# Strassen's scheme for v and u of the first batch in the second MLP

## The chip, the cores and the metric

One Trainium2 chip, one of its cores. The metric is the device time of one execution in microseconds (us), the median of several runs. The engines of the core are named as the profile names them: PE (matmuls) with PEld (its weight loads), DVE (VectorE), ACT (ScalarE), POOL (GpSimd) and SP, which issues DMAs.

## The reference

Four batches of 576 tokens go through causal attention with decay (8 heads of 64), a first MLP (512 to 2048 to 512, with a layer norm before and a residual), and a second MLP, which is what the change touches:

```python
def _moe2_ref(x, w_in, w_spatial, b_spatial, w_out):
    h = np.maximum(x @ w_in, 0.0)                     # 576 x 1024 per batch
    u, v = (h[..., :512], h[..., 512:])
    mu = np.mean(v, axis=-1, keepdims=True)
    var = np.mean((v - mu) ** 2, axis=-1, keepdims=True)
    v_n = (v - mu) / np.sqrt(var + 1e-06)
    v_s = np.einsum('ts,bsd->btd', w_spatial, v_n) + b_spatial[None, :, None]
    return ((u * v_s) @ w_out).astype(np.float32)
```

## The kernel before

Every large product is made of float16 halves: a float32 matrix X is scaled by a power of two and split into X = Xh + Xl, both float16 (`halves`, L933: one ACT instruction writes the high half, one DVE instruction the low half), and `mm3` (L799) makes three matmuls of each block, Ah·Bl, Al·Bh and Ah·Bh.

The first MLP runs in eight groups of tokens; its last group (blocks 7 and 8, 512 columns a matmul, 16 steps of 24 matmuls) runs from about 492 to 575 us. Beside its matmuls, `load_m2` (L947) loads and splits what the second MLP needs: w_in (its v half first, then its u half; raw in the tile `win`), the first 512 tokens of batch 0 (`load_x2(0)`, L990; raw `x2r`, halves `x2h` and `x2l`), w_spatial (`load_ws`; raw tile `wsr`, halves `wsh` and `wsl`) and w_out (raw `wor`, halves `woh` and `wol`). At its end it forms the four sums of blocks of w_in's u half that Strassen's scheme wants (L981 to L988: four DVE additions, then four splits, into `wuh` and `wul`).

`mlp2(b)` (L1089) is the second MLP of one batch. For batch 0 it makes, in this order: v of tokens 0 to 511 in four tiles of 128 tokens (`vtile`, 12 matmuls of 512 columns each, a ReLU on ACT, mean and variance on DVE, the reciprocal root on ACT and DVE, normalisation on DVE, split into `vh` and `vl`); u transposed, as 4 x 12 matmuls of 288 columns and 4 x 12 of 224 (`utile`, each with a ReLU on ACT); then the last 64 tokens, whose x comes late from the last group (the "tail": `split(ts)`, whose squares stand behind the last ReLU of u on ACT, `self.urelu`); v of the tail (tile 4) and u of the tail (4 x 12 matmuls of 64 columns); the spatial product z (`main`: per half of the tokens 4 x 12 matmuls of 288 columns, whose first 3 read v tile 0, the next 3 tile 1, and so on, and 2 more matmuls each for the tail and the bias); the gate, a product of u and z on DVE; and the output product with w_out. In batches 1 to 3 u already comes from `uunit` (L1143): two units of seven products of 2 x 3 matmuls of 288 columns each, in four PSUM banks A, D, B, C, three of which are used twice, with three copies on ACT and five sums on DVE per unit; the sums of blocks of x are made in `load_x2`, `whole`.

`run` interleaves the steps of the batches: after step n of `mlp2(b)`, `XN[b]` says how many steps of `load_x2(b + 1)` follow; `NEXT` steps of batch 0 run before two steps (`FILL`) of batch 1. What the code writes in this order is a priority: a planner at compile time orders the queue of each engine by it, taking, of what it holds to be ready, what stands first in the code. PSUM banks of the second MLP are taken in the order 2, 3, 4, 7, 0, 1, 5, 6 (`ORDER`).

Of the kernel before, what the change touches and what calls it, by code (L numbers as in the profile page):

```python
# [6 lines left out]
F32 = mybir.dt.float32  # L7
# [36 lines left out]
XN = ((1, 8, 13, 14, 14, 14, 15, 21, 21, 21, 21), (2, 3, 4, 5, 5, 5, 5, 14, 14, 14, 14), (1, 3, 5, 6, 6, 6, 6, 15, 15, 15, 15))  # L44
NEXT, FILL = 22, 2
# [43 lines left out]
class Kernel:  # L89
# [857 lines left out]
    def load_m2(self):  # L947
# [5 lines left out]
        self.undo_in = []  # L953
        for n, hs in enumerate((slice(DM, DF2), slice(0, DM))):
            yield from self.wide([(self.moe2_w_in[k * P : (k + 1) * P, hs], win[:, k, hs]) for k in range(NK)])
            undo, sc = self.scale16([win[:, k, hs] for k in range(NK)], f"win{n}", lambda k: self.wih[:, k, hs], up=3 - n)
            self.undo_in.append(undo)
            sc_u = sc
# [22 lines left out]
        lo, hi, spare = slice(0, 2 * P), slice(2 * P, DM), slice(DM, DF2)  # L981
        s1, s2, s3, s4 = [win[:, i, spare].rearrange("p (k m) -> p k m", k=2) for i in range(4)]
        for out, a, b, op in ((s1, win[:, :2, hi], win[:, 2:, hi], ALU.add), (s2, s1, win[:, :2, lo], ALU.subtract),
                              (s3, win[:, :2, lo], win[:, :2, hi], ALU.subtract), (s4, win[:, 2:, lo], s2, ALU.subtract)):
            nc.vector.tensor_tensor(out=out, in0=a, in1=b, op=op)
        self.wsum = [w.tile([P, 4, 2, 2 * P], F16, name=name) for name in ("wuh", "wul")]
        for i, x in enumerate((s1, s2, s3, s4)):
            self.halves(x, sc_u, self.wsum[0][:, i], self.wsum[1][:, i])  # L988

    def load_x2(self, b):  # L990
# [9 lines left out]
        def split(ts):  # L1000
            behind = (self.tlast if b == 1 else self.glast) if b else self.urelu if undo else None
            g = self.scale16_steps([x2r[:, :, ts]], f"x2s{b % 2}", lambda i: x2h[:, :, ts], behind)
            next(g)
            if b == 1:
                yield
            u, sc = next(g)
            undo.append([self.product(f"x2u{b % 2}{n}", u, self.undo_in[n]) for n in range(2)])
            if b == 1:
                yield
            for k in range(NK):  # L1010
                first = self.halves(x2r[:, k, ts], sc, x2h[:, k, ts], x2l[:, k, ts])
                if b == 0:
                    self.tlast = first
                if b == 1:
                    self.after(first, self.vlast)
                if b == 1 and ts.start == 0 and k < NK - 1:
                    yield

        def whole():
# [9 lines left out]
            a, c = slice(0, S // 2), slice(S // 2, S)  # L1029
            t = self.m2.tile([P, 4, 2, S // 2], F32, tag="x2t", name="x2t", bufs=1)  # L1030
            self.xsum = [self.m2.tile([P, 4, 2, S // 2], F16, tag=tag, name=tag, bufs=1) for tag in ("x2th", "x2tl")]
            for i, (x, y) in enumerate(((x2r[:, :2, c], x2r[:, :2, a]), (x2r[:, 2:, c], t[:, 0]), (x2r[:, 2:, c], x2r[:, :2, c]), (x2r[:, 2:, a], t[:, 1]))):
                self.after(nc.vector.tensor_tensor(out=t[:, i], in0=x, in1=y, op=ALU.subtract), self.gl)
                self.halves(t[:, i], sc, self.xsum[0][:, i], self.xsum[1][:, i])
                yield
# [11 lines left out]
        yield from split(slice(0, 512))  # L1047
        yield
        if b == 0:
            nc.sync.dma_start(out=x2r[:, :, ts], in_=self.tail(self.x2_d, b, N - 512))  # L1050
        yield
        yield from split(ts)

    def load_ws(self):
# [3 lines left out]
        raw = w.tile([P, 5, S], F32, name="wsr")  # L1058
# [30 lines left out]
    def mlp2(self, b):  # L1089
# [22 lines left out]

        def vtile(i):

            lo, hi = i * P, (i + 1) * P
            pv = bank()
# [4 lines left out]
            st = m2.tile([P, 6], F32, tag="bst", name="bst", bufs=3)  # L1121
            mv = m2.tile([P, 2], F32, tag="mv", name="mv", bufs=3)
            y = m2.tile([P, 2], F32, tag="vy", name="vy", bufs=3)
            nc.vector.bn_stats(out=st, in_=v)
            nc.vector.bn_aggr(out=mv, in_=st)
            nc.scalar.activation(y[:, 0:1], mv[:, 1:2], AF.Ln, bias=self.eps)
            nc.scalar.activation(y[:, 0:1], y[:, 0:1], AF.Exp, scale=-0.5)
            nc.vector.tensor_tensor(out=y[:, 1:2], in0=y[:, 0:1], in1=y[:, 0:1], op=ALU.mult)
            nc.vector.scalar_tensor_tensor(out=y[:, 1:2], in0=mv[:, 1:2], scalar=EPS, in1=y[:, 1:2], op0=ALU.add, op1=ALU.mult)
            nc.vector.tensor_scalar(out=y[:, 1:2], in0=y[:, 1:2], scalar1=-0.5, scalar2=1.5, op0=ALU.mult, op1=ALU.add)  # L1130
            nc.vector.scalar_tensor_tensor(out=y[:, 0:1], in0=y[:, 0:1], scalar=2.0**VS, in1=y[:, 1:2], op0=ALU.mult, op1=ALU.mult)
            nc.vector.tensor_scalar(out=v, in0=v, scalar1=mv[:, 0:1], scalar2=y[:, 0:1], op0=ALU.subtract, op1=ALU.mult)
            return v

        def utile(dt, *cols):
            ds_, c0, c1 = slice(dt * P, (dt + 1) * P), cols[0][0], cols[-1][1]
            pu = bank()
            for k in range(NK):
                self.mm3(pu[:, : c1 - c0], self.wih[:, k, ds_], self.wil[:, k, ds_], x2h[:, k, c0:c1], x2l[:, k, c0:c1], k == 0, k == NK - 1)
            for a, e in cols:  # L1140
                self.urelu = nc.scalar.activation(u[:, dt, a:e], pu[:, a - c0 : e - c0], AF.Relu, scale=undo[a // 512][1])

        def uunit(m):  # L1143

            lo, hi = slice(m * P, m * P + P), slice((m + 2) * P, (m + 3) * P)
            t1, t2 = slice(0, HS), slice(HS, S)
            (sh, sl), (th, tl) = self.wsum, self.xsum
            A, D, B, C = [bank()[:, :HS] for _ in range(4)]

            def old(k, ms):  # L1150
                return self.wih[:, k, ms], self.wil[:, k, ms]

            def new(i, k):
                return sh[:, i, k, lo], sl[:, i, k, lo]

            def x(k, ts):
                return x2h[:, k, ts], x2l[:, k, ts]

            def t(i, k):
                return th[:, i, k], tl[:, i, k]  # L1160

            def product(out, w, x, start):
                for k in range(2):
                    self.mm3(out, *w(k), *x(k), start and k == 0, k == 1, skip_group_check=True)

            def part(tag):
                return m2.tile([P, HS], F32, tag=tag, name=tag, bufs=2)

# [361 lines left out]
```

## Time and profile before

| | us |
|---|---|
| median of 3 runs | 771.42 |
| lowest, highest | 769.38, 771.96 |
| the profiled execution | 774.42 |
| its span, first to last instruction | 772.6 |

The time of an execution holds the span and about 1.8 us around it. PE's work is listed twice, as matmuls (PE) and weight loads (PEld). A timeline row gives the start, the time taken (of all instructions merged in the row), engine, line, operation, output and inputs with shapes; a bracket tells the idle time before and what ended it. Where rows overlap, the spacing of their starts is the cost of one more instruction, and the time taken is its latency.

### The profile page before, as it was taken

What the parts mean: (1) busy time and instruction counts of PE and PEld (TensorE: products, weight loads), DVE (VectorE), ACT (ScalarE), POOL (GpSimd) and SP (SyncE); (2) the same over time, 40 slices, a digit from 0 to 9 for tenths busy, and PEclk for the clock granted to TensorE, in tenths of its full rate; (3) what the DMA queues carried; (4) which work ended last, traced back from release to release, by engine and by line L of the source; (5) the groups of instructions that cost most, each with busy time, mean ns of one, the idle gap of its engine ahead of it and who ended that gap; (6) DMA issues with size and microseconds to landing.
All of it is one profiled execution on the core that took longest, in us unless ns stands there. A gap on an engine that the chain in (4) does not pass through costs nothing.

```text
span 772.6 us, 16271 instructions
## 1 busy us (share of the span) xinstructions
PE 747.0 (97%) x5924; PEld 573.0 (74%) x5924; DVE 584.9 (76%) x1549; ACT 528.1 (68%) x1318; POOL 67.2 (9%) x102
## 2 busy tenths in 40 slices
PE   8899998999998999999999999999999999999998
PEld 7788887888876787877878888644447668768676
DVE  7999799576589679979958964779534697785854
ACT  6898599576689588888958853477335765755633
POOL 6001101013101001101200200200012000000000
PEclk9999999999999899999999999999999999999999
DMA  8978793377589799997974874741015230000101
GB/s 264 296 255 295 242 215 71 73 180 124 171 160 170 186 183 174 198 215 159 200 184 102 127 112 143 197 153 56 1 20 110 70 97 28 31 32 1 62 2 62
DMA packets 164099, 104.68 MB, mean 135 GB/s; under 512 B 106146, under 2 KB 151298, under 8 KB 164020
## 3 DMA queue, kind: packets, MB, share of 16 engines
q1 hardware_dynamic: 157784, 96.60, 50.5%
q0 software_dynamic: 5376, 5.54, 5.6%
q10 hardware_dynamic: 860, 1.52, 0.6%
q8 instruction: 46, 0.75, 0.4%
q14 instruction: 33, 0.27, 0.1%
HBM read 64.37 MB, written 15.11 MB: 103 GB/s over the span
## 4 chain that ended last, share of the span: by engine, by line
PE 65%; DVE 13%; ACT 9%; DMA 8%; issue 3%; SPq 1%; DVEq 0%; ACTq 0%
PE ph L858 16%; PE acc L843 13%; PE pb L802 8%; PE pb L803 8%; PE pb L804 8%; PE s L359 3%; PE av L582 2%; DMA vr<-in_v_dram 2%; DMA raw<-in_moe_w_ch_dram 2%; PE s L843 2%; DVE wt L741 1%; DMA raw<-in_moe_w_in_dram 1%; DMA x2z<-decay_d 1%; DVE P L380 1%; ACT P L319 1%
## 5 line engine op out<-in xcount | busy, mean ns | idle before, releaser
L843 PE MATMUL acc<-hh,wt 128*128 128x256 f16 (+2 forms) x960 | 197.6, 296 | 3.0 <-ACT hh L869 2.9
L858 PE MATMUL ph<-xh,wt 128*128 128x256 f16 (+1 forms) x896 | 186.8, 290 | 4.2 <-DVE hl L873 4.1
L858 PEld LDWEIGHTS <-wt 128*128 128x128 f16 x1344 | 127.5, 99 | 50.3 <-issue 12.7
L843 PEld LDWEIGHTS <-wt 128*128 128x128 f16 x1344 | 129.0, 98 | 44.3 <-issue 5.8
L858 PE MATMUL ph<-xl,wt 128*128 128x256 f16 (+1 forms) x448 | 129.6, 289 | 0.0
L843 PE MATMUL acc<-hl,wt 128*128 128x256 f16 (+1 forms) x416 | 116.1, 283 | 0.6 <-DVE hl L873 0.6
L869 ACT ACTIVATE hh<-ph 128x256 f16<-128x256 f32 (+2 forms) x128 | 50.8, 397 | 55.7 <-PE ph L858 55.4
L873 DVE SCALAR_TENSOR_TENSOR hl<-ph,hh 128x256 f16<-128x256 f32 (+1 forms) x112 | 50.7, 454 | 42.2 <-ACT hh L869 41.8
L319 ACT ACTIVATE P<-sd,st 128x512 f16<-128x512 f32 (+1 forms) x128 | 70.0, 585 | 8.5 <-DVE st L370 5.2
L380 DVE SCALAR_TENSOR_TENSOR P<-sd,st,P 128x384 f16<-128x384 f32 (+1 forms) x96 | 58.6, 631 | 11.1 <-ACT P L319 10.2
L367 ACT ACTIVATE sd<-sd,st 128x384 f32<-128x384 f32 (+2 forms) x80 | 54.5, 682 | 13.3 <-DVE st L363 13.1
L359 PE MATMUL s<-x2z 128*128 128x384 f32 (+3 forms) x128 | 48.6, 388 | 6.1 <-DMA x2z<-decay_d 4.2
L363 DVE CUSTOM_DVE_ANT_0 sd<-s,mask 128x384 f32<-128x384 f32 (+2 forms) x80 | 46.0, 580 | 4.7 <-PE s L359 4.0
L894 POOL DMA_DIRECT2D x_d<-t x36 | 32.0, 1042 | 194.0 <-DVE t L890 162.3
L359 PE MATMUL s<-x 128*128 128x384 f32 (+3 forms) x128 | 42.4, 340 | 0.0
L804 PE MATMUL pb<-wsh,vh 128*128 128x288 f16 x128 | 36.6, 286 | 0.0
L803 PE MATMUL pb<-wsl,vh 128*128 128x288 f16 x128 | 36.6, 286 | 0.0
L802 PE MATMUL pb<-wsh,vl 128*128 128x288 f16 x128 | 36.6, 286 | 0.0
L804 PE MATMUL pb<-gh,woh 128*128 128x288 f16 x128 | 35.0, 286 | 0.0
L803 PE MATMUL pb<-gl,woh 128*128 128x288 f16 x128 | 34.9, 286 | 0.0
L802 PE MATMUL pb<-gh,wol 128*128 128x288 f16 x128 | 33.3, 286 | 0.0
L916 ACT ACTIVATE gh<-u 128x288 f16<-128x288 f32 x32 | 14.0, 438 | 26.6 <-DVE u L1255 25.4
(332 smaller groups left out, 1691.7 us busy)
## 6 DMA issues: line engine op xcount, KB each, us to landing
raw<-in_moe_w_ch_dram SPq DMA_DIRECT2D x32, 512.0 KB
qk<-in_qk_dram SPq DMA_DIRECT2D x32, 448.0 KB
vraw<-in_v_dram SPq DMA_DIRECT2D x5, 1024.0 KB
vr<-in_v_dram SPq DMA_DIRECT2D x16, 320.0 KB
x_d<-xT SPq DMA_DIRECT2D x9, 512.0 KB
x_d<-t POOLq DMA_DIRECT2D x36, 128.0 KB, 4.3
out_dram<-o SPq DMA_DIRECT2D x32, 144.0 KB
raw<-in_moe_w_in_dram SPq DMA_DIRECT2D x8, 512.0 KB
```

The source lines that it names most:

```text
L319: self.nc.scalar.activation(out, in_, AF.Copy, scale=scale)
L359: nc.tensor.matmul(ps[: R * u + R, : c1 - c0], lhsT=x[:, lo - q0 - R * u : hi - q0], rhs=y[:, c0:c1], start=g == 0, stop=g == len(heads[u] ...
L363: nc.vector.tensor_tensor_reduce(out=sd[:M, c0:c1], in0=ps[:M, : c1 - c0], in1=mask, scale=-0.125, scalar=3e38 if n == 0 else st[:M, n - 1 ...
L367: nc.scalar.activation(sd[:M, :N], sd[:M, :N], AF.Exp, bias=st[:M, n : n + 1], scale=-1.0, accum_out=st[:M, 2:3])
L380: low = nc.vector.scalar_tensor_tensor(out=dl, in0=src, scalar=rs, in1=dh, op0=ALU.mult, op1=ALU.subtract)
L802: first = mm(out, lhsT=al, rhs=bh, start=start, stop=False, **kw)
L803: mm(out, lhsT=ah, rhs=bl, start=False, stop=False, **kw)
L804: mm(out, lhsT=ah, rhs=bh, start=False, stop=stop, **kw)
L843: ins = nc.tensor.matmul(acc[m], lhsT=a, rhs=b, start=bank not in clear, stop=last and e == len(terms) - 1, skip_group_check=True)
L858: ins = nc.tensor.matmul(ph, lhsT=a, rhs=b, start=k == e == 0, stop=k == NK - 1 and e == len(terms) - 1)
L869: relu = nc.scalar.activation(hh, ph, AF.Relu)
L873: nc.vector.scalar_tensor_tensor(out=hl, in0=ph, scalar=0.0, in1=hh, op0=ALU.max, op1=ALU.subtract)
```

## The change

For batch 0, v and u of the first 512 tokens are each made as seven products of half-size blocks in place of eight: token halves of 256, halves of the inner dimension of 256, halves of v's or u's columns of 256. `uunit` becomes `seven`, which serves v and u: `vunit(n)` gives v tiles n and n + 2 at once, `uunit(m)` two of u's four column tiles. Each matmul has 256 columns. For that `load_m2` makes the four block sums of w_in's v half too (in the first 512 columns of four rows of `wsr`, once its halves are made), and the four block sums of x of batch 0 (`sums`, in the raw tile of w_out, once its halves are made), and splits them (the halves of x's sums are kept where w_in's raw u half was). Norms of two v tiles share their small instructions. u of batch 0 is now kept without ReLU and scaled by w_spatial's factor; the gate takes the maximum with 0, as in the other batches. The tail's squares stand behind the copy `five` of the last u unit. The scales of x and w_in leave one or two more powers of two of headroom for the sums. There are 17 steps of batch 0 in place of 24, and `XN[0]` and `NEXT` name the same places in the new count. The tile `v` has four buffers in place of three.

```diff
-XN = ((1, 8, 13, 14, 14, 14, 15, 21, 21, 21, 21), (2, 3, 4, 5, 5, 5, 5, 14, 14, 14, 14), (1, 3, 5, 6, 6, 6, 6, 15, 15, 15, 15))
-NEXT, FILL = 22, 2
+XN = ((1, 4, 6, 7, 7, 7, 8, 14, 14, 14, 14), (2, 3, 4, 5, 5, 5, 5, 14, 14, 14, 14), (1, 3, 5, 6, 6, 6, 6, 15, 15, 15, 15))
+NEXT, FILL = 15, 2
...
-        lo, hi, spare = slice(0, 2 * P), slice(2 * P, DM), slice(DM, DF2)
-        s1, s2, s3, s4 = [win[:, i, spare].rearrange("p (k m) -> p k m", k=2) for i in range(4)]
...
+        self.wsum = []
+        for n, c in enumerate((DM, 0)):
+            lo, hi = slice(c, c + 2 * P), slice(c + 2 * P, c + DM)
+            if n:
+                s = [win[:, i, DM:].rearrange("p (k m) -> p k m", k=2) for i in range(4)]
+            else:
+                s = [self.wsr[:, i, : 4 * P].rearrange("p (k m) -> p k m", k=2) for i in range(4)]
+            for out, a, b, op in ((s[0], win[:, :2, hi], win[:, 2:, hi], ALU.add), (s[1], s[0], win[:, :2, lo], ALU.subtract),
+                                  (s[2], win[:, :2, lo], win[:, :2, hi], ALU.subtract), (s[3], win[:, 2:, lo], s[1], ALU.subtract)):
+                nc.vector.tensor_tensor(out=out, in0=a, in1=b, op=op)
+            self.wsum.insert(0, [w.tile([P, 4, 2, 2 * P], F16, name=f"ws{n}{name}") for name in "hl"])
+            for i in range(4):
+                self.halves(s[i], scales[n], *(t[:, i] for t in self.wsum[0]))
+        t = [wout[:, i].rearrange("p (k m) -> p k m", k=2) for i in range(4)]
+        x = win.rearrange("p k d -> p (k d)").bitcast(F16).rearrange("p (i r k m) -> p i r k m", i=4, r=4, k=2)
+        for _ in self.sums0(t, [x[:, :, 0], x[:, :, 1]]):
+            pass
...
-            behind = (self.tlast if b == 1 else self.glast) if b else self.urelu if undo else None
+            behind = self.five if undo else None
...
+        def sums(sc, t, halves, behind=None):
+            self.xsum = halves
+            w = S // 2 if b else TOK
+            a, c = slice(0, w), slice(w, 2 * w)
+            for i, (x, y) in enumerate(((x2r[:, :2, c], x2r[:, :2, a]), (x2r[:, 2:, c], t[0]), (x2r[:, 2:, c], x2r[:, :2, c]), (x2r[:, 2:, a], t[1]))):
+                added = nc.vector.tensor_tensor(out=t[i], in0=x, in1=y, op=ALU.subtract)
+                if behind is not None:
+                    self.after(added, behind)
+                self.halves(t[i], sc, halves[0][:, i], halves[1][:, i])
                 yield
...
-            v = m2.tile([P, DM], F32, tag="v", name="v", bufs=3)
             nc.scalar.activation(v, pv, AF.Relu, scale=undo[min(i // 4, len(undo) - 1)][0])
...
+        def seven(w, x, scale, c11, c12, c21, c22, relu):
+
+            A, D, B, C = [bank()[:, :half] for _ in range(4)]
+            one, five, two, three = [part(tag, HS)[:, :half] for tag in ("one", "five", "two", "three")]
+
+            def product(out, a, b, start):
+                for k in range(2):
+                    (wh, wl), (xh, xl) = w(a, k), x(b, k)
+                    args = (xh, xl, wh, wl) if relu else (wh, wl, xh, xl)
+                    self.mm3(out, *args, start and k == 0, k == 1, skip_group_check=True)
+
+            def add(out, bank, other):
+                nc.vector.scalar_tensor_tensor(out=out, in0=bank, scalar=scale, in1=other, op0=ALU.mult, op1=ALU.add)
+
+            product(A, "11", "11", True)
+            nc.scalar.activation(one, A, AF.Copy, scale=scale)
+            product(D, 0, 0, True)
+            self.five = nc.scalar.activation(five, D, AF.Copy, scale=scale)
+            product(B, 1, 1, True)
+            add(two, B, one)
+            product(C, 2, 2, True)
+            add(three, C, two)
+            product(A, "21", "21", False)
+            nc.scalar.activation(c11, A, AF.Relu if relu else AF.Copy, scale=scale)
+            product(D, 3, "22", False)
+            add(c12, D, two)
+            product(C, "22", 3, False)
+            nc.vector.tensor_tensor(out=c22, in0=three, in1=five, op=ALU.add)
+            add(c21, C, two)
...
+        def vunit(n):
+
+            a, b = part("v", bufs=4), part("v", bufs=4)
...
+            seven(wblock, lambda i, k: block(x2, xsum, i, k, lambda c: slice(c * TOK + n * P, c * TOK + (n + 1) * P)), undo[0][0],
+                  a[:, :TOK], b[:, :TOK], a[:, TOK:], b[:, TOK:], True)
+            nc.scalar.activation(a[:, TOK:], a[:, TOK:], AF.Relu)
+            nc.scalar.activation(b, b, AF.Relu)
+            return a, b
 
         early = b == 0
...
+        for tiles in ((0, 2), (1, 3)) if early else ((0,), (1,), (2,), (3,)):
+            vs = vunit(tiles[0]) if early else [vtile(*tiles)]
+            norm(*vs)
+            for i, v in zip(tiles, vs):
+                nc.scalar.activation(vh[:, i, :], v, AF.Copy)
+                nc.vector.tensor_tensor(out=vl[:, i, :], in0=v, in1=vh[:, i, :], op=ALU.subtract)
             yield
         u = m2.tile([P, NK, S], F32, tag="u", name="u", bufs=1)
-        for dt in range(NK if early else 0):
-            utile(dt, (0, HS))
-            yield
+        self.su = [self.product(f"su{b % 2}", undo[0][1], self.wsc[:, 0])]
         if early:
-            for dt in range(NK):
-                utile(dt, (HS, 512))
+            for m in range(2):
+                uunit(m)
+                yield
             for _ in self.x2_0:
                 pass
...
```

## Rows read from the trace of the kernel before

**Rows 1.** Page, part 1: busy time (share of the span) and count of each engine.
```profile
PE 747.0 (97%) x5924; PEld 573.0 (74%) x5924; DVE 584.9 (76%) x1549; ACT 528.1 (68%) x1318; POOL 67.2 (9%) x102
```
**Rows 2.** Windows: length, busy us per engine (instructions), granted TensorE clock, DMA share, GB/s.
```profile
518.00:535.00 17.00, 16.53 (x80) 7.64 (x78) 16.60 (x33) 12.98 (x27) 0.00 (x0) 1.00 0.26 90
...
550.00:574.00 24.00, 24.00 (x114) 11.02 (x113) 7.22 (x14) 4.83 (x8) 0.00 (x0) 1.00 0.00 1
...
576.00:596.40 20.40, 20.40 (x143) 13.80 (x142) 9.25 (x32) 10.94 (x27) 6.44 (x8) 1.00 0.70 123
596.40:611.00 14.60, 14.60 (x150) 11.12 (x149) 5.94 (x25) 10.20 (x28) 0.00 (x0) 1.00 0.30 91
611.00:650.00 39.00, 38.89 (x283) 27.45 (x282) 37.47 (x100) 27.05 (x66) 0.00 (x0) 1.00 0.21 62
650.00:772.60 122.60, 119.11 (x897) 87.20 (x894) 78.01 (x211) 62.59 (x156) 0.00 (x0) 1.00 0.09 30
```
**Rows 3.** Waits of PE from 470 us to the end: who, total, times, longest.
```profile
PE ph L858 <- DVE hl L873: 0.3, 1, 0.3
```
**Rows 4.** Timeline of PE: the stall, then the first matmul of each stage of batch 0.
```profile
523.94 0.38 PE L858 MATMUL ph<-xh,wt 128*128 128x512 f16 x1 [0.34 <-DVE hl L873]
...
575.57 0.38 PE L802 MATMUL pb<-wih,x2l 128*128 128x512 f16 x1
...
585.92 0.29 PE L802 MATMUL pb<-x2h,wil 128*128 128x288 f16 x1
...
591.80 0.26 PE L802 MATMUL pb<-x2h,wil 128*128 128x224 f16 x1
...
596.40 0.29 PE L802 MATMUL pb<-wsh,vl 128*128 128x288 f16 x1
```
**Rows 5.** Timeline of PE in the first MLP: first of ten 256-column matmuls, and what follows.
```profile
491.20 0.27 PE L843 MATMUL acc<-hl,wt 128*128 128x256 f16 x1
...
492.30 0.59 PE L858 MATMUL ph<-xh,wt 128*128 128x512 f16 x2
```
**Rows 6.** Timeline of DVE beside the last group of the first MLP.
```profile
521.66 1.29 DVE L985 TENSOR_TENSOR win<-win 128x512 f32<-128x512 f32 x2
...
523.20 0.69 DVE L873 SCALAR_TENSOR_TENSOR hl<-ph,hh 128x512 f16<-128x512 f32 x1
...
545.91 3.00 DVE L1081 SCALAR_TENSOR_TENSOR wsl<-wsr,wsc,wsh 128x576 f16<-128x576 f32 x4 [0.66 <-ACT wsh L1080]
...
561.53 2.74 DVE L935 SCALAR_TENSOR_TENSOR wol<-wor,wout,woh 128x512 f16<-128x512 f32 x4 [0.60 <-ACT woh L934]
```
**Rows 7.** Timeline of ACT: three high halves of the sums of w_in.
```profile
533.12 1.94 ACT L934 ACTIVATE wuh<-win,win 128x512 f16<-128x512 f32 x3
```
**Rows 8.** Timelines of DVE and ACT: 256 columns read from PSUM.
```profile
488.12 0.43 DVE L873 SCALAR_TENSOR_TENSOR hl<-ph,hh 128x256 f16<-128x256 f32 x1 [0.24 <-ACT hh L869]
...
487.70 0.38 ACT L869 ACTIVATE hh<-ph 128x256 f16<-128x256 f32 x1 [0.73 <-PE ph L858]
```
**Rows 9.** Timelines of ACT and DVE: v tile 3, from ReLU to low half.
```profile
589.93 0.68 ACT L1120 ACTIVATE v<-pb,x2u 128x512 f32<-128x512 f32 x1
...
590.65 0.69 DVE L1124 BATCH_NORM_STATS2 bst<-v 128x6 f32<-128x512 f32 x1
...
593.40 0.55 DVE L1132 TENSOR_SCALAR v<-v,mv,vy 128x512 f32<-128x512 f32 x1
594.64 0.69 DVE L1195 TENSOR_TENSOR vl<-v,vh 128x512 f16<-128x512 f32 x1 [0.69 <-ACT vh L1194]
```
**Rows 10.** Timelines of SP, ACT, DVE and PE: the tail's load, squares, low halves, first matmul.
```profile
585.29 0.38 SPq L1050 DMA_DIRECT2D x2r<-x_d  x1
...
596.95 0.62 ACT L916 ACTIVATE x2h<-x2r 128x512 f16<-128x512 f32 x1
...
599.07 1.23 DVE L935 SCALAR_TENSOR_TENSOR x2l<-x2r,x2s,x2h 128x128 f16<-128x128 f32 x4
...
601.07 0.38 PE L802 MATMUL pb<-wih,x2l 128*128 128x512 f16 x1
```

More of the change, by code (lines that the diff above doesn't have):

```diff
@@ L1000, in split @@
         def split(ts):
-            behind = (self.tlast if b == 1 else self.glast) if b else self.urelu if undo else None
-            g = self.scale16_steps([x2r[:, :, ts]], f"x2s{b % 2}", lambda i: x2h[:, :, ts], behind)
+            behind = self.five if undo else None
+            g = self.scale16_steps([x2r[:, :, ts]], "x2s0", lambda i: x2h[:, :, ts], behind, up=3 if undo else 2)
             next(g)
-            if b == 1:
-                yield
-            u, sc = next(g)
-            undo.append([self.product(f"x2u{b % 2}{n}", u, self.undo_in[n]) for n in range(2)])
-            if b == 1:
-                yield
[L1010 to L1017, printed above, removed]
+            u, sc = next(g)
+            undo.append([self.product(f"x2u0{n}", u, self.undo_in[n]) for n in range(2)])
+            for k in range(NK):
+                self.tlast = self.halves(x2r[:, k, ts], sc, x2h[:, k, ts], x2l[:, k, ts])
+            return sc
+        def sums(sc, t, halves, behind=None):
[7 more added lines that the diff above has]
+                self.halves(t[i], sc, halves[0][:, i], halves[1][:, i])
+                yield
         def whole():
@@ L1028, in whole @@
                 yield
-            a, c = slice(0, S // 2), slice(S // 2, S)
             t = self.m2.tile([P, 4, 2, S // 2], F32, tag="x2t", name="x2t", bufs=1)
[L1031 to L1035, printed above, removed]
+            halves = [self.m2.tile([P, 4, 2, S // 2], F16, tag=tag, name=tag, bufs=1) for tag in ("x2th", "x2tl")]
+            yield from sums(sc, [t[:, i] for i in range(4)], halves, self.gl)
         for u in range(2):
@@ L1046, in load_x2 @@
             return
-        yield from split(slice(0, 512))
+        sc = split(slice(0, 512))
+        self.sums0 = lambda t, halves: sums(sc, t, halves)
         yield
-        if b == 0:
-            nc.sync.dma_start(out=x2r[:, :, ts], in_=self.tail(self.x2_d, b, N - 512))
+        nc.sync.dma_start(out=x2r[:, :, ts], in_=self.tail(self.x2_d, b, N - 512))
         yield
-        yield from split(ts)
+        split(ts)
     def load_ws(self):
@@ L1057, in load_ws @@
         self.wsl = w.tile([P, 5, S], F16, name="wsl")
-        raw = w.tile([P, 5, S], F32, name="wsr")
+        raw = self.wsr = w.tile([P, 5, S], F32, name="wsr")
         ss = w.tile([P, 6], F32, name="wss")
@@ L1128, in vtile @@
[L1128 to L1132, printed above, removed]
@@ new lines, in block, with whole, tile @@
+        def block(pair, sums, i, k, cols):
+            if isinstance(i, str):
+                c = cols(int(i[1]) - 1)
+                return [t[:, 2 * int(i[0]) - 2 + k, c] for t in pair]
+            return [t[:, i, k, cols(0)] for t in sums]
+        x2, win, xsum, (wsu, wsv) = (x2h, x2l), (self.wih, self.wil), self.xsum, self.wsum
+        def whole(c):
+            return slice(c * half, (c + 1) * half)
+        def uunit(m):
+            def tile(c):
+                return slice(c * TOK + m * P, c * TOK + (m + 1) * P)
+            seven(lambda i, k: block(win, wsu, i, k, tile), lambda i, k: block(x2, xsum, i, k, whole), self.su[0],
+                  u[:, m, whole(0)], u[:, m, whole(1)], u[:, m + 2, whole(0)], u[:, m + 2, whole(1)], False)
@@ L1220, in mlp2 @@
         vt1, vt2 = self.vt1[b % 2], self.vt2[b % 2]
-        for dt in range(NK if early else 0):
-            utile(dt, (512, S))
-            yield
         for m in range(0 if early else 2):
             uunit(m)
+            yield
+        if early:
+            for dt in range(NK):
+                utail(dt)
             yield
```

103 lines of the change are left out of this document (33 added, 70 removed).

## Prediction

> **What bounds the kernel now.** I read the busy shares first, then the windows, then the waits of PE, then the timelines around the change. PE is busy for 97% of the span [rows 1], and the windows show it full from 500 us on: in the stages from 550 to 611 us not a tenth of a microsecond is missing, from 611 to 650 us 0.11 us, and what is missing after 650 us (3.5 us) is the run-out at the end [rows 2]. The clock is granted in full (1.00, the 2.4 GHz level) throughout [rows 2]. From 470 us to the end the list of PE's waits has a single entry, 0.3 us [rows 3]; it is the stall at 523.94 [rows 4]. So in this part the time is the sum of PE's matmuls, and a matmul less is time less, as long as nothing else becomes late. Two other readings matter: DVE is full in two stages, 518 to 535 us (16.60 of 17) and 611 to 650 us (37.47 of 39), and has room in three, 550 to 574 us (7.22 of 24), 576 to 596.4 us (9.25 of 20.4) and 596.4 to 611 us (5.94 of 14.6) [rows 2].
>
> **Matmuls.** v takes from 575.57 to 585.92, 10.35 us for 48 matmuls of 512 columns (0.216 us each); u takes from 585.92 to 596.40, 5.88 us for 48 of 288 columns (0.1225 each) and 4.60 us for 48 of 224 (0.0958 each): 20.83 us in all [rows 4]. After the change v and u are two units each of seven products of 2 x 3 matmuls with 256 columns: 4 x 42 = 168 matmuls. Ten such matmuls take 492.30 - 491.20 = 1.10 us in the first MLP, 0.110 each [rows 5]; half way between the 224 and 288 columns lies 0.109. That makes 18.5 or 18.3 us. The saving is 2.35 to 2.49 us; I take 2.4.
>
> In the rows a matmul with half the columns costs half, so the eighth that is saved in products is saved in time. The Trainium skill, "TensorE: Matmul & The Clock Gate", section "Back-to-back issue gap", speaks against this: for streams of weight loads and matmuls it gives about 81 ns at 128 columns and 131 ns at 512, and calls N/2.4 + 2.5 ns an isolated figure that over-counts wide matmuls. Estimated from that page, with a straight line between its two figures, 256 columns would cost 98 ns, v would go from 6.3 to 8.2 us, u from about 9.4 to 8.2, and the change would lose 0.7 us. The trace disagrees, with 216 ns at 512 columns.
>
> **Sums made ahead, beside the last group of the first MLP.** Removed from the full stage 518 to 535 us and just behind it are the four DVE sums of w_in's u half (0.65 us each) and their splits [rows 6]; they move, since their scratch now becomes free only when the v half's sums are read. The stall at 523.94 stands right behind two of these sums, which delayed the low half `hl` that PE waited for [rows 4, 6]. I credit 0.3 us for it, with bounds 0 and 0.47 (all that PE lacks in that window [rows 2]).
>
> Added behind 549 us, when the last of w_spatial's raw rows has been read (545.91 + 3.00 [rows 6]): sums of w_in's v half, then of its u half, then of x. That is 12 sums x 0.65 = 7.8 us and 12 splits at 2.74 per four = 8.2 us of DVE, 16.0 us, where 24 - 7.22 = 16.8 us are free [rows 2, 6]. ACT gets 12 high halves x 0.65 = 7.8 us where 19 us are free [rows 2, 7]. The sums of x are last: their scratch is w_out's raw tile, read until 561.53 + 2.74 = 564.3 [rows 6]. Queue on DVE: v and u sums and splits, 10.7 us, and three `hl` of 0.69 from 549 reach 562; w_out's splits reach 565; x's sums, splits and one more `hl` 2.6 + 2.74 + 0.69 reach 571. The first matmul that needs them is the second product of v, at 575.57 + 6 x 0.11 = 576.2. So I cost this at nothing, with 5 us of cover. If the cover is gone, each microsecond beyond 576.2 is one of PE, less little. `hl` stands behind at most one such sum more, 0.7 us, and is used two steps (10 us) later: nothing.
>
> **Beside v and u (576 to 594 us).** Per unit PE's banks are emptied by three ACT copies of 0.38 us and four DVE sums of 0.43 us, and DVE adds one sum without PSUM, which I also take at 0.43 [rows 8]. Four units are 20 x 0.43 = 8.6 us of DVE; norms of four tiles stay (0.69 + 0.55 + 0.69 each for the long ones [rows 9]), half of the small instructions go. By DVE's busy time of before, 9.25 us [rows 2], DVE comes to nearly 18 us in the 18.4 that PE takes. ACT loses four ReLUs of 0.68 and eight of u, gets 12 copies of 0.38 and the ReLUs on sums: about the same as its 10.94 us. Inside the units PE has cover: the four units need nothing of one another, and a bank used again by product 5, 6 or 7 was filled three products (2 us) before; its reader needs 0.4 us and at most one long DVE instruction (0.69) ahead of it. I cost this at nothing, up to 0.5 us.
>
> Behind the units stands z, whose fourth matmul reads v tile 1. The second v unit ends on PE at 575.57 + 9.2 = 584.8, u at 593.9 to 594.1. In between tiles 1 and 3 need: the last sum 0.43, two ReLUs 0.38 + 0.68, statistics to normalisation as in tile 3 of before (593.40 - 590.65 = 2.75) and 0.69 more for the second tile, normalisation to the end of the low half (594.64 + 0.69 - 593.40 = 1.93) and 1.24 more [rows 8, 9]: 8.1 us alone, so 593.1 at best. With DVE nearly full, sums of u stand between; of their ten (4.3 us) some fall into the time in which the chain is on ACT. z can begin with the parts that read tile 0 (2 x 3 matmuls of 0.12, 0.7 us). I take a wait of 0.6 us; bounds 0 (all hidden) and 4.8 (all ten sums and the tail's 1.23 [rows 10] ahead: 593.1 + 5.5 - 593.9).
>
> **The tail.** Its load is issued at 585.29, but its squares waited on ACT for the last ReLU of u until 596.95, and v tile 4 began at 601.07 [rows 10]. Now they stand behind `five` of the last unit, some 3 us before u ends; the same 4.1 us of chain ends at about 595 or 596, 3 us or more before 601.07 - 2.4, so tile 4 can only help fill PE. Steps of batch 1 keep their places: SP's queue and POOL's have the same instructions in the same order. Behind it, the gate costs the same. The DVE stage of 611 to 650 us moves ahead with PE, as its first inputs are z and x of batch 1, both earlier.
>
> **Sum.** -2.4 (matmuls) - 0.3 (stall at 523.94) + 0.6 (start of z) = -2.1 us. Against the profiled execution, 774.42 with a span of 772.6, that gives 772.3. The profile lies 3.0 us above the median of the runs, 771.42, more than the change itself, so I carry over the difference: 769.3.
>
> **Rivals.**
> Everything is hidden: z does not wait. For it: the chain of tiles 1 and 3 alone would end at 593.1, before u does, and the sums of u can fall into its time on ACT. Time: -2.4 - 0.3, at most -2.49 - 0.47, so 768.5 to 768.7.
> z waits 2 us or more for tiles 1 and 3, as DVE becomes the bound of this stage. For it: the near-full DVE. Against: tile 4 and three parts of z can go first. At a wait of 2.7 the gain is nil; at the bound of 4.8 it is 773.5. Time 771.5.
> DVE is already the bound from 611 to 650 us: what PE gains, it gives back waiting there. For it: 96% busy [rows 2]. Against: DVE has 8.7 us free just before [rows 2], so it can start earlier. Time 771.1, the stall's 0.3 alone.
> On the slower side: the sums of x are late. They stand last on a DVE that has 0.8 us to spare in 550 to 574 us, behind w_out's splits. If the planner puts them behind the last group's outputs, 2.6 + 2.74 us from 576 on, PE finds the second product unready at 576.2 and waits some 5.1 us until 581.3: 771.4 - 2.7 + 5.1 = 773.8. It is a loss from a lateness of 2.7 us, thus if x's splits end behind 578.9, 8 us later than I have them.
> The matmuls are not shorter in step with their columns: at 20.83 / 168 = 0.124 us each the products gain nothing, and with z's 0.6 us the time is 772.0. Against: 0.110 in [rows 5]. The Trainium skill's page on TensorE, cited above, is on this side.
>
> **How the numbers follow.** Forecast 0.42, everything hidden 0.22, z waits 0.17, DVE from 611 us 0.11, x's sums late 0.07, matmuls not shorter 0.01. A measurement of this kernel can tell about 0.3%, 2.3 us, from no change; that is below 769.1 and above 773.7. The forecast stands just inside it, so I count 0.18 of its 0.42 as faster, with all of the second case: faster 0.40. Slower: 0.06 of the late sums and 0.03 of z's waits: 0.09. The rest, 0.51, is within. The range goes from 767.4 (768.5 and a microsecond for the scatter of the runs, which spread over 2.6 us) to 772.6, which takes in the waits of z up to some 4 us and leaves out the late sums.
>
> **What would show it.** Right: 168 matmuls of 256 columns at 0.109 to 0.110 us between 573 and 592; the row at 523.94 without its bracket; x's sums on DVE ending before 573; tile 4's first matmul less than 4 us behind the end of u; all later stages 2 us earlier. Wrong: a PE wait on `vl` or `vh` of over a microsecond at the start of z, on the halves of x's sums at 576, or on a `two` or `three` within the units; or a new PE wait on DVE between 608 and 650 us.

## The result, and the profile after

The changed kernel is slower. Beside 22 executions of the kernel before (median 771.31 us) 22 of it gave 775.68 us, ratio 1.0051, 95% interval 1.0036 to 1.0067; in a second series 12 gave 774.03 against 771.34 (29), ratio 1.0030 (1.0011 to 1.0049). I had forecast 769.3, in a range from 767.4 to 772.6.

Profiles are compared here from v's first matmul to the end of the span, because the time up to v scatters: v begins at 575.57 and 573.09 us in two traces of before and at 569.23 and 570.60 in two of after, with the same instructions in the same order in every queue as far as the last group of the first MLP. Behind v one kernel repeats itself within 0.1 us:

| kernel | v's first matmul | span | from v to the end |
|---|---|---|---|
| before, two traces | 575.57, 573.09 | 772.6, 770.1 | 197.03, 197.01 |
| after, two traces | 569.23, 570.60 | 769.1, 770.4 | 199.87, 199.80 |

So 2.84 us are lost behind v where I expected a gain of 1.8 (-2.4 and +0.6). 2.84 us is 0.37% of 771.3, inside both intervals, though at the lower edge of the first: there the medians lie 4.4 us apart, and the traced execution of after, 770.87 us, is the shortest of its 22. The loss is looked for behind v; what the first series has beyond 2.84 us comes up again at the end of the experiments.

The windows of after, columns as in [rows 2]: the stretch that answers to 518 to 535, the one beside the end of the first MLP, then v's start to the end of the first wait, on to z's last wait, on to the gate, and the 38 us behind:

```profile
512.00:529.00 17.00, 16.87 (x82) 7.89 (x80) 15.57 (x32) 12.14 (x27) 0.00 (x0) 1.00 0.26 89
543.66:567.66 24.00, 24.00 (x114) 11.04 (x113) 21.71 (x38) 13.05 (x20) 0.00 (x0) 1.00 0.00 1
569.23:581.00 11.77, 9.94 (x90) 8.63 (x89) 4.61 (x11) 4.45 (x11) 7.35 (x9) 1.00 0.82 92
581.00:593.90 12.90, 10.53 (x91) 8.58 (x91) 11.66 (x39) 8.35 (x23) 0.00 (x0) 1.00 0.38 110
593.90:607.80 13.90, 13.47 (x137) 10.06 (x138) 6.82 (x26) 9.67 (x26) 0.00 (x0) 1.00 0.33 97
607.80:646.00 38.20, 38.15 (x278) 27.15 (x278) 34.97 (x96) 26.05 (x65) 0.00 (x0) 1.00 0.21 63
```

PE, without a gap in these stages before, lacks 1.83, 2.37 and 0.43 us in the third to fifth. And DVE, the engine with more to do, is busy for only 4.61 of the first 11.77 us, then for 11.66 of 12.90. The list of PE's waits from 463 to 640 us, one entry in [rows 3], now reads:

```profile
PE pb L802 <- DVE vl L1226: 1.9, 2, 1.3
PE pb L802 <- ACT v L1179: 1.9, 1, 1.9
PE pb L802 <- DVE u L1285: 0.5, 1, 0.5
PE pb L802 <- DVE u L1168: 0.5, 1, 0.5
```

Their places are on the timelines of PE (first row, the largest wait) and of PEld (the other rows: the idle time of the weight loads, which holds no modelled end of a matmul and so is nearer to what the wait costs):

```profile
581.03 0.27 PE L802 MATMUL pb<-x2h,wil 128*128 128x256 f16 x1 [1.86 <-ACT v L1179]
...
581.03 0.10 PEld L803 LDWEIGHTS <-wih 128*128 128x128 f16 x1 [2.04 <-issue]
590.51 0.10 PEld L802 LDWEIGHTS <-vl 128*128 128x128 f16 x1 [0.83 <-DVE vl L1226]
592.04 0.10 PEld L803 LDWEIGHTS <-vh 128*128 128x128 f16 x1 [0.65 <-issue]
593.88 0.10 PEld L802 LDWEIGHTS <-vl 128*128 128x128 f16 x1 [1.62 <-DVE vl L1226]
607.85 0.10 PEld L803 LDWEIGHTS <-vh 128*128 128x128 f16 x1 [0.67 <-issue]
```

They add up to 5.81 us. Less the matmuls saved (2.49, below), and less the one idle time that before has here (0.42, below), that is 2.90 us, against 2.84 measured. The account closes within 0.1 us: matmuls saved, waits added. In before that idle time stands in front of x of batch 1, on PEld:

```profile
614.82 0.10 PEld L802 LDWEIGHTS <-x2l 128*128 128x128 f16 x1 [0.42 <-DVE x2l L935]
```

**The first wait.** PE waits at 581.03 for L1179, the copy `c11` of the first v unit, which has to empty a bank that the first u unit takes over. ACT's timeline shows what stood ahead of it, POOL's what that was waiting for:

```profile
573.42 0.47 ACT L1173 ACTIVATE five<-pb,x2u 128x256 f32<-128x256 f32 x1 [0.18 <-PE pb L804]
579.34 1.14 ACT L1116 ACTIVATE vt<-on 64x512 f16<-64x512 f32 x2 [5.44 <-POOL on L1114]
580.51 0.47 ACT L1179 ACTIVATE v<-pb,x2u 128x256 f32<-128x256 f32 x1
...
569.03 2.66 POOL L894 DMA_DIRECT2D x_d<-t  x3 [64.56 <-DVE t L890]
...
577.85 0.85 POOL L894 DMA_DIRECT2D x_d<-t  x1 [0.91 <-PE pb L804]
578.74 0.57 POOL L1114 MEMSET on<- 64x576 f32 x1
```

ACT stands idle for 5.44 us with products in PSUM to be read. At the head of its queue are the two copies of a constant into `vt2` (L1116), which z's bias wants only some 25 us later (the first matmul with `vt` runs at 605.74). They wait for POOL's memset of `on`, and that stands behind the eight DMAs which write the first MLP's last outputs, issued by POOL at 0.85 to 0.89 us each, with gaps: 9.7 us from the first issue to the memset. Both instructions are in the kernel before too, and the same rows of its ACT and POOL show why they cost nothing there:

```profile
583.54 0.69 ACT L1120 ACTIVATE v<-pb,x2u 128x512 f32<-128x512 f32 x1 [1.90 <-PE pb L804]
584.55 1.14 ACT L1109 ACTIVATE vt<-on 64x512 f16<-64x512 f32 x2 [0.33 <-POOL on L1107]
...
583.94 0.57 POOL L1107 MEMSET on<- 64x576 f32 x1
```

The memset ends 8.9 us behind v's first matmul there, and 10.1 after. But in before the planner had put the copies behind a ReLU at 583.54, 8 us into v, so they waited 0.33 us; in after they stand behind the fourth small copy, 4.2 us into v.

**The waits at the start of z.** DVE's timeline in after: idle while ACT is held up, then, from 582.20 until z has its last tile, one instruction behind another (of the rows left out before it one has a bracket, 1.11 us; of those behind it none):

```profile
576.04 0.48 DVE L1168 SCALAR_TENSOR_TENSOR v<-pb,x2u,two 128x256 f32<-128x256 f32 x1 [1.08 <-PE pb L804]
...
582.20 1.29 DVE L1139 BATCH_NORM_STATS2 bst<-v 128x6 f32<-128x512 f32 x2 [2.77 <-ACT v L1215]
...
593.99 0.68 DVE L1226 TENSOR_TENSOR vl<-v,vh 128x512 f16<-128x512 f32 x1
```

Of z's three waits the first (0.83) ends with the low half of v tile 0, the second (0.65) with a sum of the last u unit, whose bank z takes over, the third (1.62) with the low half of tile 1: all three are work that stands in this full queue.

### The profile page after: what moved, and what is told of

Read it like the earlier page. It is cut to its first block, busy times and chain, and to the rows that moved or that the text cites. A ratio compares the mean times of both kernels' runs of the same rounds, so it can differ in the third digit from the quotient of the medians.

```text
span 769.1 us, 16364 instructions
## 1 busy us (share of the span) xinstructions
PE 741.1 (96%) x5948; PEld 572.5 (74%) x5948; DVE 600.5 (78%) x1579; ACT 533.9 (69%) x1326; POOL 67.4 (9%) x102
## 4 chain that ended last, share of the span: by engine, by line
PE 55%; issue 12%; DVE 11%; DMA 9%; ACT 9%; SPq 1%; POOL 1%; POOLq 0%; ACTq 0%; DVEq 0%
PE ph L858 12%; PE acc L843 11%; PE pb L802 7%; PE pb L804 7%; PE pb L803 7%; PE s L359 4%; DMA vr<-in_v_dram 3%; PE av L582 3%; DMA raw<-in_moe_w_ch_dram 2%; DVE wt L741 1%; ACT P L319 1%; DMA qk<-decay 1%; DMA x2z<-decay_d 1%; POOL x_d L894 1%; ACT sd L367 1%
```

## The experiments

Three theories, as the expectations name them. A: the place of the two copies is all of the loss. B: besides, DVE has more to do in this stage than there is time for, so z waits whatever the order. C: DVE's work would fit, but its order, and PE's mixing of the two v units, bring it late.

**No copies** (`e1_no_copy`). POOL sets the constant in `vt2` itself; `on` and the two ACT copies go:

```diff
-            on = m2.tile([P, S], F32, tag="raw", name="on", bufs=2)
-            nc.gpsimd.memset(on[64:], 2.0**VS)
             for t in self.vt2:
-                nc.scalar.activation(t[64:], on[64:, :DM], AF.Copy)
+                nc.gpsimd.memset(t[64:], 2.0**VS)
```

> The changed kernel, but the two constant rows of vt2 are written by POOL straight into their float16 tiles, so that ACT has no copy of them and never stands behind POOL. Theory A (ACT's queue: its two copies stand in front of the units' copies and wait 5.4 us for POOL's memset, which stands behind eight DMA issues): PE's wait of 1.9 us at the second u unit goes, and z's waits (2.3 us) fall below 1 us; from the first matmul of v to the end of the span 195 to 196 us where the change has 199.9 and before 197.0; time 0.995 of before. Theory B (DVE is full, so z waits for tiles 1 and 3 whatever ACT does): the wait of 1.9 us goes, z's 2.3 us stay; 198 us from v to the end, time 1.002 of before.

Measured: 770.88 against 770.48 us, ratio 1.0012 (0.9994 to 1.0031); 770.9 - 573.60 = 197.30 us from v to the end. The wait for `c11` is gone, and 2.57 of the 2.84 us with it; neither A's 195 to 196 nor B's 198 was met. What is left stands at the start of z and at the gate, on PEld:

```profile
593.06 0.10 PEld L803 LDWEIGHTS <-vh 128*128 128x128 f16 x1 [0.44 <-issue]
594.97 0.10 PEld L803 LDWEIGHTS <-vh 128*128 128x128 f16 x1 [1.56 <-issue]
...
609.67 0.10 PEld L803 LDWEIGHTS <-vh 128*128 128x128 f16 x1 [0.86 <-issue]
```

Its windows, v's start to 583.88 and on to 597.40, show DVE idle for more than half of the first stretch and full in the second:

```profile
573.60:583.88 10.28, 10.28 (x95) 9.09 (x94) 4.60 (x11) 4.83 (x12) 7.72 (x10) 1.00 0.84 95
583.88:597.40 13.52, 11.89 (x106) 9.85 (x105) 13.32 (x44) 9.46 (x25) 0.00 (x0) 1.00 0.42 115
```

The two instructions on that full DVE behind whose ends z's matmuls start at 593.06 and 594.97, 0.05 to 0.06 us later:

```profile
592.86 0.15 DVE L261 TENSOR_SCALAR x2s<-pb 128x1 uint32<-128x1 uint32 x1
...
594.44 0.47 DVE L1166 SCALAR_TENSOR_TENSOR u<-pb,su,two 128x256 f32<-128x256 f32 x1
```

One reads the tail's sum of squares, the other is the last sum of u; both empty a bank that z takes over. So here z waits for banks, and not for v tiles 1 and 3. (The list of waits puts the longer one down to `x2s` at L262, which reads no PSUM and ends no earlier than the matmul starts.)

**The same edit in the kernel before** (`e2_before_no_copy`), to see whether the copies cost anything there.

> The kernel before with the same edit. Theory A: there the copies waited 0.3 us for POOL and PE never felt it, so nothing changes: 197.0 us from v to the end, give or take 0.3, ratio 0.999 to 1.001. Rival: the copies cost ACT time that counts in both kernels, and before gains 1 us too.

Measured: 770.72 against 770.48, ratio 1.0006 (0.9989 to 1.0023); 197.05 us from v to the end, as before. The copies cost only where the change put them.

**The copies, later in the queue** (`e8_copies_later`): both the memset and the copies stay, and the copies stand behind the last ReLU of the second v unit.

```diff
-            for t in self.vt2:
-                nc.scalar.activation(t[64:], on[64:, :DM], AF.Copy)
+            constant = [nc.scalar.activation(t[64:], on[64:, :DM], AF.Copy) for t in self.vt2]
...
-            nc.scalar.activation(b, b, AF.Relu)
+            relu = nc.scalar.activation(b, b, AF.Relu)
+            if n:
+                for ins in constant:
+                    self.after(ins, relu)
```

> The changed kernel with its two ACT copies of the constant kept, and POOL's memset that they need kept as well, but the copies set behind the last ReLU of the second v unit in ACT's queue. Theory A (it is the place in the queue that costs: the copies stand behind four copies of the first v unit, and wait there until POOL has issued its eight transfers): from v's first matmul to the end of the span 197.3 us, as without any copies, up to 197.8 for the copies' own 0.6 us on ACT; PE's wait of 1.9 us for c11 of the first v units gone. Rival (it is the copies' own work, or POOL's memset beside DVE): 199.8 as in the changed kernel.

Measured, in one execution: 769.7 - 573.03 = 196.67 us, 3.2 less than after; the copies run without a wait:

```profile
584.18 1.15 ACT L1115 ACTIVATE vt<-on 64x512 f16<-64x512 f32 x2
```

So it is the place, not the work. That it comes out 0.6 us below the kernel without copies was not expected: the planner ordered other things anew too (the gate's wait is gone, z's waits are 1.20 on `vl`, 0.40 and 1.02 on the tail).

**Both once more** (`before_again`, `after_again`), one execution each, for the table above.

> The kernel before once more, for a second profile: v to the end again 197.0 us within 0.5 (fixed orders), while the time up to v differs by some us. Rival: it differs as the total does.

> The changed kernel once more, for a second profile. If the loss sits in fixed queue orders, ACT's wait for POOL is again 5 to 6 us and v to the end is again 199.9 us within 0.5, while the time up to v differs by some us. Rival: the stretch from v to the end differs by as much as the total does (8 us).

Measured: 197.01 and 199.80 us from v to the end, as in the first traces.

**u alone** (`e3_u_only`): no copies; v in four tiles as before, u in two units of seven products.

```diff
...
-        for n, c in enumerate((DM, 0)):
+        for n, c in ((1, 0),):
...
-        for tiles in ((0, 2), (1, 3)) if early else ((0,), (1,), (2,), (3,)):
-            vs = vunit(tiles[0]) if early else [vtile(*tiles)]
+        for tiles in ((0,), (1,), (2,), (3,)):
+            vs = [vtile(*tiles)]
```

> Without ACT's copies of the constant, and only u of batch 0 from seven products; v from eight, one tile at a time, as before. PE's matmuls are 1.3 us less than before's. Theory B (what is left of the loss is a full DVE between the second v unit and z): DVE has 4 us less there than with both, z does not wait, and from v's first matmul to the end it is 195.7 to 196.1 us, against 197.0 before and 197.3 with both; time 0.998 of before. Theory C (the planner's mixing of the units, not DVE's load, makes z wait): the two u units stand last on PE and z waits for their last sums as it does with both, 196.8 or more.

**v alone** (`e4_v_only`): no copies; v in two units of seven products, u in eight `utile` steps, with its ReLU and its gate as before.

> Without ACT's copies, and only v of batch 0 from seven products; u from eight with a ReLU on ACT, as before. PE's matmuls are 1.2 us less than before's. Theory B: the ten sums of u are gone from DVE, z does not wait, 195.8 to 196.2 us from v to the end. Theory C: tiles 1 and 3 still end late because PE mixes the two v units, z waits a microsecond, 196.8 to 197.2.

Measured: with u alone 768.99 against 770.60 us, ratio 0.9974 (0.9951 to 0.9997), 195.97 us from v to the end; with v alone 771.16, ratio 0.9999 (0.9974 to 1.0023), 196.92 us. Each saves about half of the 2.49 us. With u alone the only wait left is the gate's (0.67 us of idle PEld); with v alone there are one on `vl`, 0.57, and the gate's, 0.92. 195.97 lies in B's range (195.7 to 196.1), 196.92 in C's (196.8 to 197.2), so the pair decides for neither. Half of the change is a gain, and it is the half that leaves the v tiles early.

**The sums `c22` on POOL** (`e5_pool_sum`): no copies, and one of five sums per unit taken from DVE, which by theory B is overfull.

```diff
-            nc.vector.tensor_tensor(out=c22, in0=three, in1=five, op=ALU.add)
+            (nc.gpsimd if b == 0 else nc.vector).tensor_tensor(out=c22, in0=three, in1=five, op=ALU.add)
```

> Both parts, without ACT's copies, and the four sums of batch 0 that read no PSUM (three plus five, 0.41 us each) on POOL in place of DVE. Theory B: DVE gets 1.65 us back where it is full for 13 us, and z's waits of 2.3 us shrink by 1 to 1.65: 195.7 to 196.4 us from v to the end. Theory C: the order on PE decides, 197.0 to 197.4 as with both parts.

Measured: 774.41, ratio 1.0045 (1.0021 to 1.0069), 199.59 us from v to the end: 2.3 us worse than with all sums on DVE. POOL's timeline shows why: its first sum stands behind the same DMA issues.

```profile
582.69 0.85 POOL L894 DMA_DIRECT2D x_d<-t  x1 [0.77 <-PE pb L804]
...
584.64 1.41 POOL L1181 TENSOR_TENSOR v<-three,five 128x256 f32<-128x256 f32 x2
```

It is made 10.3 us into v (584.64, with v from 574.31), where DVE had made it 5.3 us into v without the copies. The run says nothing for or against B; it shows the first cause a second time.

**The products in the order of the code** (`e9_in_order`): no copies, and each of the 28 products of v and u of batch 0 on PE behind the one before.

```diff
...
-                    self.mm3(out, *args, start and k == 0, k == 1, skip_group_check=True)
+                    ins = self.mm3(out, *args, start and k == 0, k == 1, skip_group_check=True)
+                    if early and k == 0 and self.third0 is not None:
+                        self.after(ins, self.third0)
+                self.third0 = self.third
```

> As the kernel without the copies, and the 28 products of v and u of batch 0 run on PE in the order of the code, each behind the one before, where the planner had mixed the units. Theory C (the mixing makes the first v tiles late, so that DVE first stands idle and then is full until z starts): z's waits for its bank and its tiles shrink from 2.1 us to under 0.6, 195.0 to 195.6 us from v's first matmul to the end of the span, ratio to the kernel before 0.997. Theory B (DVE simply has more work in this stage than time, in whatever order): 197.0 to 197.5 as with the mixed order, ratio 1.001. A loss is possible too: products in strict order wait for banks and sums (over 198).

Measured: 771.31 against 771.67 us, ratio 0.9988 (0.9964 to 1.0013); 770.6 - 574.62 = 195.98 us, 1.32 less than with the mixed order. z does not wait any more. DVE's busy time in the first 10.28 us has grown from 4.60 to 7.30 us, in the 13.50 behind them it has sunk to 11.99:

```profile
574.62:584.90 10.28, 10.28 (x95) 9.08 (x94) 7.30 (x21) 5.88 (x15) 7.41 (x9) 1.00 0.81 92
584.90:598.40 13.50, 12.46 (x111) 10.65 (x110) 11.99 (x36) 8.76 (x24) 0.93 (x2) 1.00 0.44 118
```

One new wait keeps it above C's 195.0 to 195.6. On PE, and then on DVE:

```profile
588.99 0.27 PE L802 MATMUL pb<-win,wil 128*128 128x256 f16 x1 [1.04 <-DVE three L1169]
...
587.27 1.28 DVE L1137 BATCH_NORM_STATS2 bst<-v 128x6 f32<-128x512 f32 x2
588.47 0.47 DVE L1169 SCALAR_TENSOR_TENSOR three<-pb,su,two 128x256 f32<-128x256 f32 x1
```

The sum `three`, which empties a bank that PE needs again two products later, stands behind two statistics of 0.6 us each.

**Three places on DVE as well** (`e10_stats_later`): those statistics behind `three`, the second v unit's normalisation ahead of the last unit's `two`, the last split of `vt` behind the first gate (in part; the two notes behind # are not in the code).

```diff
...
+            if early and not relu and not self.moved:
+                self.after(self.stats, added)      # added: the sum `three`
+                self.moved = True
...
+            if early and not relu and self.moved:
+                self.after(added, self.normed)     # added: the sum `two`
...
+                if early and hf == dt == 0:
+                    self.after(split, gate)
```

> As the kernel with the products in order, with three places on DVE moved as well: the statistics of the second v unit behind the sum `three` of the first u unit (PE had waited 1.04 us for that sum, which stood behind them), the normalisation of that v unit ahead of the sum `two` of the last u unit, and the last split of the tail's v behind the first gate (PE had waited 0.48 us there). Theory C (order on DVE, not its load, makes what is lost): both waits go, 194.4 to 194.9 us from v's first matmul to the end of the span, ratio 0.996 to 0.997. Theory B (the load: a wait removed comes back at the next instruction that DVE is late with): 195.8 to 197.

Measured: 769.20 against 771.34 us, ratio 0.9972 (0.9957 to 0.9986): the whole change, faster than both kernels. 765.3 - 569.93 = 195.37 us from v to the end. Both waits are gone, 1.9 us of idle PEld; 0.6 is gained, since a new wait of 1.08 us has come, at the start of z for the last unit's `two`, which I had myself put behind the normalisation:

```profile
589.03 0.28 PE L802 MATMUL pb<-wsh,vl 128*128 128x288 f16 x1 [1.08 <-DVE two L1170]
```

195.37 lies between C's 194.4 to 194.9 and B's 195.8 to 197. So C named the larger part: order on PE and DVE is worth 1.9 us (197.30 to 195.37). Whether the last microsecond is DVE's load, as B has it, or only the order that I set, no run separates.

**The times once more** (`after_five`, `e3_again`), in one series.

> The changed kernel once more, for its time. If what the profiles show behind v's first matmul (2.84 us, less 0.47 for the stall at 523.94) is all of the loss, the ratio is 1.003; if something ahead of v costs 1.6 us more, it is 1.005 again.

> The kernel with Strassen's products for u alone and without the copies, once more, for its time. From the profiles, 195.97 against 197.03 us behind v's first matmul and 0.47 for the stall ahead of it, it should be 1.5 us faster than before, ratio 0.998; at its first measurement 0.9974.

Measured: after 774.03, ratio 1.0030 (1.0011 to 1.0049), so nothing ahead of v is needed to explain the loss of this series; u alone 768.81, ratio 0.9962 (0.9940 to 0.9983), 195.94 us from v to the end. In the same series the whole change in its best order took 769.20, so its 0.6 us less in the trace do not show in the times. This third trace of after shows something else, though: 201.20 us from v to the end, 1.3 more than the first. The stretch that starts with z's last wait shows where:

```profile
596.30:611.80 15.50, 15.08 (x137) 10.77 (x138) 6.75 (x25) 9.61 (x25) 0.00 (x0) 0.89 0.29 87
```

Granted clock 0.89. On PE's timeline the matmuls of 288 columns start 0.12 us apart, then 0.24, then 0.12 again:

```profile
596.61 0.29 PE L802 MATMUL pb<-wsh,vl 128*128 128x288 f16 x1
596.73 0.29 PE L803 MATMUL pb<-wsl,vh 128*128 128x288 f16 x1
...
597.43 0.44 PE L804 MATMUL pb<-wsh,vh 128*128 128x288 f16 x1
597.67 0.44 PE L802 MATMUL pb<-wsh,vl 128*128 128x288 f16 x1
...
600.59 0.29 PE L802 MATMUL pb<-wsh,vl 128*128 128x288 f16 x1
600.72 0.29 PE L803 MATMUL pb<-wsl,vh 128*128 128x288 f16 x1
```

From 596.98 to about 600.4 PE ran at the lower of its two levels, 1.2 GHz. What it had done before: four waits, 1.54, 0.56, 0.47 and 1.32 us, the last three within 5 us of that point. The first trace, with the same waits and 1.86 for the first, has 1.00 in the same stretch. From the last wait to the gate's it took 15.63 us here and 13.97 there: 1.66 us. That it is a second price of the waits is argued, not shown: it is one fall in one trace. The mean granted clock of the whole executions points the same way: in the first series the three of after at 1.000 took 770.87, 771.82 and 773.07 us, the 19 at 0.993 to 0.998 had a median of 776.19. But the kernel before falls too, well ahead of v (0.97 from 175.57 to 275.57 us in its first trace), and where the untraced executions fell is not known. So what the first series lost beyond 2.84 us stays open.

## Why the prediction was wrong

**Matmuls: right.** The term was 168 matmuls of 0.109 to 0.110 us. On PE's timeline of after:

```profile
572.57 0.27 PE L802 MATMUL pb<-ws0h,win 128*128 128x256 f16 x1
...
573.88 0.27 PE L802 MATMUL pb<-ws0h,win 128*128 128x256 f16 x1
```

12 of them in 1.31 us, 0.109 each: 18.34 us where 20.83 were [rows 4], a saving of 2.49, the upper bound. The rival that they would not shorten falls (its 772.0 also left out the 0.3 us of the stall).

**The stall at 523.94: a small term that is hardly there.** PE's 16.87 of 17 us in after against 16.53 [rows 2] looks like the 0.3 us credited. But a second trace of before has 16.80 there and no bracket. The stall belonged to that execution more than to the kernel.

**The sums made ahead: right.** DVE is busy for 21.71 of 24 us beside the first MLP's end, with no wait of PE on it. The last splits of x's sums:

```profile
564.10 1.40 DVE L935 SCALAR_TENSOR_TENSOR win<-wor,x2s,win 128x512 f16<-128x512 f32 x2
```

They end at 565.5, 4.4 us before the second product asks for them at 569.9; I had 5. The slower rival, x's sums late, is not what happened, though slower it was.

**ACT beside v and u: the step that failed.** "About the same as its 10.94 us" and "I cost this at nothing, up to 0.5 us" compare ACT's busy time. It was no bound: without the copies it had 14.29 us to do in the 23.80 around v and u. What failed was a place in a queue. I wrote that POOL's queue has the same instructions in the same order, which is true, and did not ask who waits for POOL: ACT does, for a constant, with a cover of 0.33 us in before. With v's four long ReLUs replaced by many small copies, the place at which the planner sets that constant moved from 8 us into v to 4, while POOL needed 9.0 us from its first issue to the memset in before and 9.7 after. The price is not the copies' 1.14 us but the 5.4 us in which ACT, and DVE behind it, did nothing: 2.57 to 3.2 us of PE by the two experiments. It was in no rival, and no bound of mine contained it. Why the planner put it there (it may have held `on` ready earlier than POOL's issues let it be) no row shows.

**z's wait: the size was off, within its bounds.** I took 0.6 of 0 to 4.8 (my own terms add up to 592.9 and not 593.1, and so to a bound of 4.5); without the copies it is 2.0 us of idle PEld (0.44 and 1.56), in after 3.10. The total of DVE was about right: "nearly 18 us", and 4.60 + 13.32 = 17.92 in the two windows above, which reach 5 us further than v and u. But I set it against the stage as a whole. DVE can start only when products are there: the planner mixed the two v units, the first unit's tiles were complete late, and 5.7 us of DVE were lost in the first 10.28. The rest, 13.3 us of it, then had 13.5 us, and z stood at its end. The rival "z waits 2 us or more" had the size and the bound, DVE, but only part of the mechanism: it had z wait for tiles 1 and 3, and of the 3.10 us in after 1.62 are for tile 1, of the 2.0 without the copies nothing; the rest is for tile 0 and for banks that DVE had still to read. That its 771.5, no change against 771.42, fits the ratio of 1.0012 without the copies is thus in part luck.

**The tail: costed as a help only, and its sign was not met.** Tile 4's first matmul was to come less than 4 us behind the end of u; in after it came at 596.95, 7.3 us behind the start of u's last matmul (589.68), as its scale (`x2s`, 590.84 to 593.14) and its low halves (from 594.59) stood in the same full queue of DVE. No wait of PE in after is for the tail; without the copies the 0.44 us are, for the bank of its sum of squares.

**The gate: costed as the same, a little wrong.** In after 0.67 us of idle PEld at the first gate, which the split of `vt` (0.69) held up, in place of before's 0.42 at x of batch 1: some 0.25 us.

**DVE from 611 us on: right.** 34.97 of 38.20 us busy and PE lacks 0.05; what PE loses it loses earlier.

Sum, from v to the end: +2.57 us for the copies, as the two traces differ; without them -2.49 for the matmuls, +2.0 for z and +0.86 - 0.42 at the gate make -0.05, where the trace has +0.27 (197.30 against 197.03). These 0.3 us were not placed.

## What to carry to other kernels

When a change replaces long instructions by many short ones on an engine, follow every instruction on that engine that is *not* part of the change: a constant, a copy or a load whose wait was covered by the long ones may now stand ahead of what everybody needs, and behind a queue (here eight DMA issues of POOL) that is no faster than before. Busy time against the length of a stage says little where the work becomes ready bit by bit: ask when the first piece is complete, and what stands last before the consumer. And where only half of a change keeps its inputs early, try that half: u alone, without the copies, gave 0.3 to 0.4% with none of the reordering that the whole change needed.

## What the runs showed of the hardware

POOL needs 0.85 to 0.89 us for each of these DMA issues and up to 0.9 us more between them, 9.7 us for eight; anything on POOL behind them, a memset of 0.57 us too, is that late.

With a sum of two tensors on POOL, a DVE instruction of 128x2 elements took 0.69 us; an equal one earlier took 0.15 (DVE's and POOL's timelines with `c22` on POOL):

```profile
591.41 0.15 DVE L1144 SCALAR_TENSOR_TENSOR vy<-vy 128x2 f32<-128x2 f32 x1
...
593.77 1.28 DVE L1224 TENSOR_TENSOR vl<-v,vh 128x512 f16<-128x512 f32 x2
594.98 0.69 DVE L1144 SCALAR_TENSOR_TENSOR vy<-vy 128x2 f32<-128x2 f32 x1
...
593.93 1.72 POOL L1181 TENSOR_TENSOR u<-three,five 128x256 f32<-128x256 f32 x1 [3.62 <-DVE vy L1143]
```

POOL's sum took 1.72 us there, 0.7 in its other places. The two `vl` ahead, which also read two tensors beside that sum, kept their length (1.28 us for two): whatever was shared, it was POOL and then the small instruction that lost time. The Trainium skill, "GPSIMD Engine Reference", section "1. Specifications", says that POOL shares its way into SBUF with VectorE and contends with DVE instructions that read two SBUF inputs; these rows are in line with it, on one instance.

The clock fell to its lower level for 3.4 us behind waits of half a microsecond to 1.5 us in one of three traces of after; the other two have the same waits at z and, by their 199.87 and 199.80 us, no such fall.
